# Float64 weights: the sign from GpSimd, the join and the elementwise work on VectorE, and other times for loads and conversions

## The chip, the cores and the metric

The kernel runs on one core of one Trainium2 chip. The metric is the device time of one execution in microseconds (us); the time of before is the median of three runs, 909.39 us (908.66 to 910.81). The engines are named as in the profile: PE is TensorE, DVE is VectorE, ACT is ScalarE, POOL is GpSimd and SP is SyncE. PEld is TensorE's loading of weights.

## The reference, cut to what matters

Three layers follow each other over 2304 tokens. The first is a masked attention (4 batches, 8 heads, 576 positions). The second is a feed-forward layer whose gate and output weights are drawn as float32 and divided by a square root that numpy holds in float64, so the weights reach the kernel as float64:

```python
xn = x / rms * rms_g
g = xn @ w_gate
silu = g * (1.0 / (1.0 + np.exp(-g)))
val = xn @ w_val
x = (silu * val @ w_out).astype(np.float32)
```

The third layer routes each token to one of eight experts. It is not touched by the change.

## The kernel before, in words

[...] The pieces of work:

- `load_w(n)` (L377) starts the load of weight n from ACT's queue. `next_load` (L413) calls it behind `mark`, the latest exp of the attention or tanh of the feed-forward layer, on ACT.
- `conv_a(n)` (L383): ACT scales the high word as a float32 (L388), and DVE shifts the low word right by 29 (L389).
- `conv_b(n)` (L391): DVE shifts the scaled word left by 3 and joins it with the low bits (L394), then takes the sign bit from the scaled word and joins it in (L398).
- `conv_c(n)` (L403): ACT rounds to the high part (L406), and POOL subtracts to get the low part (L407).
- These make a list of 73 pieces, `conv` (L420): a of 0, b of 0, then a of n together with c of n - 1, then b of n. `convert()` (L427) takes the next piece, and passes over every fourth call; with `LEAD` it calls for loads ahead of the pieces. `weight(n)` (L439) takes pieces until weight n is there.

The buffers of `raw`, of the work words `wk` and of the finished weight lie in a row of slots: weight n is loaded into slot n + 3, its work words lie in slot n + 2, the finished parts in slot n. So the work words of n replace the raw words of n - 1, and must wait until these have been read.

The order of the program is this. 24 units of attention run first (`att_sequence`, L250): each is scores with mask and exp (L155), division by the sum (`norm`, L201, its multiplication on POOL at L208), transposition and output. When the loop at L684 has reached unit 7 (26 pieces of attention), three more pieces and `rms0`, the normalisation of the first 256 tokens, follow. Then the flow (L1059) goes through 108 steps, 12 slices of the feed-forward width for each of nine chunks of 256 tokens; the first two chunks alternate and share the weights as they come, so that the 36 weights are wanted within the first 24 steps. A step is `gate_val` twice (24 matmuls of 256 columns, L458 to L460), `gelu_post` (L462: tanh on ACT, two DVE operations L467 and L468, rounding on ACT at L471, the rest `hl` on POOL at L472), `ff_out` of the step two before (six matmuls of 512 columns, L483 to L485), and three calls of `slot` (L722). A slot calls `next_load` and `convert` and then one piece of the attention or of the routing. `rms` for the later chunks subtracts on POOL for chunks 1 and 2 and on DVE otherwise (L353). Experts follow from the middle of the last chunk on.

The order on each engine isn't the program's: a planner places the instructions of this part in the order in which its own cost model finds them ready, the earlier of the program first. On the chip each engine then works through its list in that fixed order.

Of the kernel before, what the change touches and what calls it, by code (L numbers as in the profile page):

```python
# [10 lines left out]
F32 = mybir.dt.float32  # L11
# [5 lines left out]
ALU = mybir.AluOpType  # L17
# [29 lines left out]
def moe_kernel(  # L47
# [17 lines left out]
    V, A, G, T, SP = nc.vector, nc.scalar, nc.gpsimd, nc.tensor, nc.sync  # L65
# [81 lines left out]
    def attention(u, banks):  # L147

        b, p, g = units[u]
        local = p < 2  # L150
        n, t0, nq, nk = geometry(u)
        k0 = n * nq if local else n * nq + LQ - SQ
        st = {}

        def scores():  # L155
            t = qkv_t.pop((u, 0))
            pr = pp.tile([128, 4, LK], F32, tag="pr", name="pr", bufs=3)
            mx = sm.tile([128, 4], F32, tag="mx", name="mx")
            sd = sm.tile([128, 4], F32, tag="sd", name="sd")
            sps = banks("s")  # L160
            if n_fill[0] < 16:
                n_fill[0] += 1
                fill(sps[:, 384:], 10)
            sps = sps[:, :4 * LK].rearrange("p (t k) -> p t k", k=LK)
            for i in range(n):
                for h in range(2):
                    hp = slice(64 * h, 64 * h + 64)
                    T.matmul(
                        sps[hp, i, :nk],
                        t[hp, i * nq:i * nq + LQ],  # L170
                        t[hp, k0 + i * nq:k0 + i * nq + nk],
                        start=True,
                        stop=True,
                    )
            for i in range(n):
                mask = m_str if not local else (m_loc0 if g == 0 and i == 0 else m_loc)
                pv = pr[:, i, :nk]
                V.tensor_tensor_reduce(  # L178
                    out=pv,
                    in0=sps[:, i, :nk],  # L180
                    in1=mask[:, :nk],
                    op0=ALU.add,
                    op1=ALU.min,
                    scale=-0.125,
                    scalar=3.0e38,
                    accum_out=mx[:, i:i + 1],
                )
                act = A.activation(  # L188
                    out=pv,
                    in_=pv,  # L190
                    func=AF.Exp,
                    bias=mx[:, i:i + 1],
                    scale=-1.0,
                    accum_out=None if u < 12 else sd[:, i:i + 1],
                )
                if not flow_on:
                    mark[0] = act
            st["p"] = pr, sd
            load_part(0)

        def norm():  # L201
            pr, sd = st["p"]
            pv, sl = pr[:, :n, :nk], sd[:, :n]
            if u < 12:
                V.tensor_reduce(out=sl, in_=pv, op=ALU.add, axis=AX.X)
            V.tensor_scalar(out=sl, in0=sl, scalar1=1e-9, scalar2=None, op0=ALU.add)
            V.reciprocal(out=sl, in_=sl)  # L207
            G.tensor_tensor(out=pv, in0=pv, in1=sl.unsqueeze(2).to_broadcast([128, n, nk]), op=ALU.mult)  # L208

        def transpose():  # L210
            pr, _ = st.pop("p")
            pt = banks("t").rearrange("p (t k) -> p t k", k=128)
            for i in range(n):
                T.transpose(pt[:nk, i], pr[:, i, :nk], ident)
            ptS = st["t"] = pp.tile([128, 4, 128], F32, tag="ptS", name="ptS", bufs=2)
            A.copy(ptS[:nk, :n], pt[:nk, :n])

        def output():
            t = qkv_t.pop((u, 1))
            ptS = st.pop("t")  # L220
            ot = banks("o")
            for i in range(n):
                for h in range(2):
                    T.matmul(
                        ot[64 * h:64 * h + 64, i * nq:(i + 1) * nq],
                        t[:nk, i, 64 * h:64 * h + 64],
                        ptS[:nk, i, 64 * h:64 * h + nq],
                        start=True,
                        stop=True,
                    )  # L230
            if local:
                x = x_t[b, p, g] = xt_p.tile([128, n * LQ], F32, tag=f"x{g}", name=f"x{g}", bufs=2)
                A.copy(x, ot[:, :n * LQ])
            else:
                if g == 0:
                    x_t[b, p] = xt_p.tile([128, S], F32, tag="xs", name="xs", bufs=4)
                x = x_t[b, p].rearrange("p (j c) -> p c j", c=CLS)
                c0, c1 = 3 * t0, min(3 * (t0 + n), CLS)
                A.copy(x[:, c0:c1], ot[:, :(c1 - c0) * LEN].rearrange("p (c j) -> p c j", j=LEN))
            load_part(1)  # L240
            n_out[0] = u + 1


        if local and b > 0:
            output.after = (S * (b - 1) + LQ * (t0 + n) - 1) // CH
        elif not local and b > 1:
            output.after = (S * (b - 1) - 1) // CH
        return scores, norm, transpose, output
# [42 lines left out]
    def rms(j):  # L291
# [49 lines left out]
        def scale(q):  # L341
            y = tmp_p.tile([128, 2, CH], F32, tag="tmp", name="y")
            h = xn_p.tile([128, 2, CH], F32R, tag=f"xh{q}", name=f"xh{q}")
            l = xn_p.tile([128, 2, CH], F32R, tag=f"xl{q}", name=f"xl{q}")
            for c in range(2):
                p = 2 * q + c
                for src, o, n in segments(j, p):
                    yv, gp = y[:, c, o:o + n], g_sb[:, p:p + 1]
                    V.scalar_tensor_tensor(
                        out=yv, in0=src, scalar=gp, in1=st["r"][:, o:o + n], op0=ALU.mult, op1=ALU.mult  # L350
                    )
            A.copy(h, y)
            (G if j in (1, 2) else V).tensor_tensor(out=l, in0=y, in1=h.bitcast(F32), op=ALU.subtract)  # L353
            st[f"x{q}"] = [h[:, 0], h[:, 1]], [l[:, 0], l[:, 1]]
            if "x0" in st and "x1" in st:
                xn_t[j] = tuple(st["x0"][i] + st["x1"][i] for i in range(2))
                normed[0] = j
# [9 lines left out]
    w_t = {}  # L367
    raw_t = {}
    wk_t = {}
    sign = -(1 << 31)  # L370

    def w_slot(n, shape, dtype, name):
        if n < NP:
# [9 lines left out]
    def conv_a(n):  # L383
        wk, raw = w_slot(n + 2, [128, 2, 512], I32, "wk"), raw_t[n]
        wk_t[n] = wk


        A.activation(out=wk[:, 0].bitcast(F32), in_=raw[:, :, 1].bitcast(F32), func=AF.Copy, scale=2.0**-112)  # L388
        V.tensor_scalar(out=wk[:, 1], in0=raw[:, :, 0], scalar1=29, scalar2=None, op0=ALU.logical_shift_right)  # L389

    def conv_b(n):  # L391
        wk = wk_t[n]
        raw_t.pop(n)
        V.scalar_tensor_tensor(  # L394
            out=wk[:, 1], in0=wk[:, 0], scalar=3, in1=wk[:, 1],
            op0=ALU.logical_shift_left, op1=ALU.bitwise_or,
        )
        V.scalar_tensor_tensor(  # L398
            out=wk[:, 0], in0=wk[:, 0], scalar=sign, in1=wk[:, 1],
            op0=ALU.bitwise_and, op1=ALU.bitwise_or,  # L400
        )

    def conv_c(n):  # L403
        wk = wk_t.pop(n)[:, 0].bitcast(F32)
        w = w_t[n] = w_slot(n, [128, 2, 512], F32R, "wf")
        A.copy(w[:, 0], wk)  # L406
        G.tensor_tensor(out=w[:, 1], in0=wk, in1=w[:, 0].bitcast(F32), op=ALU.subtract)  # L407

    n_wl = [0]
    mark = [None]  # L410
# [12 lines left out]
    conv += [lambda: conv_c(NP - 1)]  # L423
    conv.reverse()

    cv = [0]
    def convert(n=1):  # L427
        cv[0] += 1
        if cv[0] % 4 == 0:
            return  # L430
        while n and conv:
            while n_wl[0] < NP and 2 * (n_wl[0] - LEAD) <= 2 * NP + 1 - len(conv):
                next_load()
            conv.pop()()
            n -= 1

    LEAD = 2

    def weight(n):  # L439
        while n not in w_t:  # L440
# [21 lines left out]
    def gelu_post(j, f):  # L462
# [6 lines left out]
        h = sl_p.tile([128, CH], F32R, tag="hh", name="hh")  # L469
        l = sl_p.tile([128, CH], F32R, tag="hl", name="hl")  # L470
        A.copy(h, t)  # L471
        G.tensor_tensor(out=l, in0=t, in1=h.bitcast(F32), op=ALU.subtract)  # L472
        hm_t[j, f] = h, l

    def ff_out(j, f):
# [186 lines left out]
        )  # L662
    V.tensor_tensor(out=bsel, in0=bsel, in1=bt, op=ALU.add)

    P0, P1, P2, P3, P4, P5 = 3, 3, 1, 4, 1, 3
    stage = [0]
    turn = {"s": 0, "t": 0, "o": 0}

# [15 lines left out]
    while n_out[0] < 8:  # L684
        aux.pop()()
        n_p += 1
        if n_p % P0 == 0 and n_wl[0] < P1 and n_p >= 15:
            next_load()
    for _ in range(P5):
        aux.pop()()  # L690
    flow_on.append(1)
    for f in rms0:
        f()
# [28 lines left out]
    def slot():  # L722
        s = now[0]
        now[0] += 1
        if s % P2 == 0:
            next_load()
        convert()
        if s in plan:
            for f in plan[s]:
                f()  # L730
        else:
            pop_aux()
# [495 lines left out]
```

## Time and profile before

| what | value |
|---|---|
| median of three runs | 909.39 us |
| the profiled execution, its own time | 910.19 us |
| its span, first to last instruction | 908.4 us |
| PE busy | 865.5 us (95%) |
| DVE busy | 503.7 us (55%) |
| ACT busy | 402.0 us (44%) |
| POOL busy | 223.7 us (25%) |
| bytes read from HBM | 91.58 MB |
| mean granted clock of TensorE | 0.974 |

The span is the part of the execution that the trace covers, and 1.8 us lie around it. Busy shares are averages over stages of different kinds: the attention at the start, the flow, and the experts. A busy PE need not be at its peak, because matmuls overlap in a pipeline; the number of matmuls in a stretch tells more.

### The profile page before, as it was taken

What the parts mean: (1) busy time and instruction counts of PE and PEld (TensorE: products, weight loads), DVE (VectorE), ACT (ScalarE), POOL (GpSimd) and SP (SyncE); (2) the same over time, 40 slices, a digit from 0 to 9 for tenths busy, and PEclk for the clock granted to TensorE, in tenths of its full rate; (3) what the DMA queues carried; (4) which work ended last, traced back from release to release, by engine and by line L of the source; (5) the groups of instructions that cost most, each with busy time, mean ns of one, the idle gap of its engine ahead of it and who ended that gap; (6) DMA issues with size and microseconds to landing.
All of it is one profiled execution on the core that took longest, in us unless ns stands there. A gap on an engine that the chain in (4) does not pass through costs nothing. (4 is left out here: it accounts for less than half of the span.)

```text
span 908.4 us, 18299 instructions
## 1 busy us (share of the span) xinstructions
PE 865.5 (95%) x6912; PEld 774.5 (85%) x6912; DVE 503.7 (55%) x1489; ACT 402.0 (44%) x970; POOL 223.7 (25%) x246
## 2 busy tenths in 40 slices
PE   8888977899999999999999999999899999999995
PEld 7676866798888898899989999998789999999994
DVE  3679999733454353362442524437586666666650
ACT  4776655325445335343232232325265555554540
POOL 1335666521112112112112111113031111111100
PEclk8889998999999999999999999999999999999998
DMA  4736860001212102110000000005187752676000
GB/s 122 221 101 235 290 243 25 1 1 39 76 32 63 52 1 60 55 35 21 24 10 17 9 1 24 1 26 207 40 303 206 226 176 74 208 233 189 30 25 19
DMA packets 33016, 84.48 MB, mean 93 GB/s; under 512 B 5122, under 2 KB 12850, under 8 KB 32920
## 3 DMA queue, kind: packets, MB, share of 16 engines
q1 hardware_dynamic: 24216, 54.89, 19.6%
q10 hardware_dynamic: 5184, 18.88, 5.8%
q0 software_dynamic: 3520, 9.45, 3.1%
q8 instruction: 58, 0.95, 0.5%
q14 instruction: 38, 0.31, 0.1%
HBM read 91.58 MB, written 10.49 MB: 112 GB/s over the span
## 5 line engine op out<-in xcount | busy, mean ns | idle before, releaser
L458 PE MATMUL gv<-xh,wf 128*128 128x256 f32 x864 | 253.4, 294 | 11.2 <-DVE t L468 10.7
L460 PE MATMUL gv<-xh,wf 128*128 128x256 f32 x864 | 247.9, 287 | 0.0
L459 PE MATMUL gv<-xl,wf 128*128 128x256 f32 x864 | 247.2, 286 | 0.1
L458 PEld LDWEIGHTS gv<-xh,wf 128*128 128x128 f32 x864 | 166.3, 193 | 21.1 <-DVE t L468 13.9
L459 PEld LDWEIGHTS gv<-xl,wf 128*128 128x128 f32 x864 | 166.5, 193 | 3.2 <-POOL xl L353 0.4
L460 PEld LDWEIGHTS gv<-xh,wf 128*128 128x128 f32 x864 | 166.5, 193 | 0.8 <-issue 0.2
L472 POOL TENSOR_TENSOR hl<-t,hh 128x256 fp32r<-128x256 f32 x108 | 86.2, 798 | 325.8 <-ACT hh L471 266.7
L946 DVE TENSOR_TENSOR l<-stg,h 128x1024 fp32r<-128x1024 f32 x88 | 107.5, 1227 | 38.7 <-ACT h L945 38.2
L467 DVE SCALAR_TENSOR_TENSOR t<-t,gv 128x256 f32<-128x256 f32 x108 | 45.2, 418 | 148.6 <-ACT t L466 148.0
L945 ACT CAST h<-stg 128x1024 fp32r<-128x1024 f32 x88 | 91.7, 1047 | 38.6 <-PE o L1002 27.6
L466 ACT ACTIVATE t<-gv 128x256 f32<-128x256 f32 x108 | 41.3, 383 | 141.2 <-PE gv L460 131.2
L471 ACT CAST hh<-t 128x256 fp32r<-128x256 f32 x108 | 43.7, 404 | 82.6 <-PE o L485 33.2
L483 PE MATMUL o<-wf,hh 128*128 128x512 f32 x192 | 76.9, 402 | 0.4 <-ACT hh L471 0.2
L484 PE MATMUL o<-wf,hh 128*128 128x512 f32 x192 | 75.9, 396 | 0.0
L485 PE MATMUL o<-wf,hl 128*128 128x512 f32 x192 | 75.6, 398 | 0.0
L1000 PE MATMUL o<-h,hT 128*128 128x512 f32 x176 | 71.1, 404 | 0.0
L1002 PE MATMUL o<-h,hT 128*128 128x512 f32 x176 | 69.1, 392 | 0.0
L1001 PE MATMUL o<-l,hT 128*128 128x512 f32 x176 | 68.7, 391 | 0.0
L929 POOL DMA_INDIRECT xg<-rows_d,gi x22 | 25.3, 1148 | 160.9 <-issue 140.3
L188 ACT ACTIVATE pr<-pr,mx 128x54 f32<-128x54 f32 (+1 forms) x160 | 52.7, 347 | 21.3 <-DVE mx L178 21.2
L407 POOL TENSOR_TENSOR wf<-wk,wf 128x512 fp32r<-128x512 f32 x36 | 51.0, 1421 | 32.0 <-ACT wf L406 30.7
L208 POOL TENSOR_TENSOR pr<-pr,sd 128x216 f32<-128x216 f32 (+4 forms) x48 | 30.0, 625 | 95.2 <-DVE sd L207 63.2
(206 smaller groups left out, 1699.1 us busy)
## 6 DMA issues: line engine op xcount, KB each, us to landing
stg<-in SPq DMA_DIRECT2D x96, 512.0 KB
raw<-in ACTq DMA_DIRECT2D x36, 512.0 KB
rows_d<-x SPq DMA_DIRECT2D x18, 256.5 KB
qk<-in SPq DMA_DIRECT2D x16, 221.0 KB
qk<-in SPq DMA_DIRECT2D x8, 272.0 KB
v<-in SPq DMA_DIRECT2D x16, 108.0 KB
qk<-in SPq DMA_DIRECT2D x8, 208.0 KB
v<-in SPq DMA_DIRECT2D x8, 192.0 KB
```

Source lines behind the costliest of these rows:

```text
L458: T.matmul(dst, wh[:, ks], xh[k], start=(k == order[0]), stop=False)
L459: T.matmul(dst, wh[:, ks], xl[k], start=False, stop=False)
L460: T.matmul(dst, wl[:, ks], xh[k], start=False, stop=(k == order[3]))
L472: G.tensor_tensor(out=l, in0=t, in1=h.bitcast(F32), op=ALU.subtract)
L483: T.matmul(o, h[:, ms], wh, start=(f == 0), stop=False)
L484: T.matmul(o, h[:, ms], wl, start=False, stop=False)
L485: T.matmul(o, l[:, ms], wh, start=False, stop=(f == NF - 1))
L945: A.copy(h, lt["stg", i])
L946: V.tensor_tensor(out=l, in0=lt["stg", i], in1=h.bitcast(F32), op=ALU.subtract)
L1000: T.matmul(ys[t][m], hh, w[0][:, c], start=(q == 0 and c == 0), stop=False)
L1001: T.matmul(ys[t][m], hh, w[1][:, c], start=False, stop=False)
L1002: T.matmul(ys[t][m], hl, w[0][:, c], start=False, stop=(q == 3 and c == 1))
```

## The change

The change moves the sign: POOL makes it in `conv_a` from the high word, as the integer of 0 or -2^31. DVE then needs two operations and no separate shift. Four subtractions and multiplications go from POOL to DVE, and the calls of `next_load` and `convert` come at other places: a load at every second piece of the attention, a piece of the conversion at every second one after the tenth, with no passing over in `convert`, and `LEAD` of 4.

```diff
@@ norm
-            G.tensor_tensor(out=pv, in0=pv, in1=sl.unsqueeze(2).to_broadcast([128, n, nk]), op=ALU.mult)
+            V.tensor_tensor(out=pv, in0=pv, in1=sl.unsqueeze(2).to_broadcast([128, n, nk]), op=ALU.mult)
@@ rms, scale
-            (G if j in (1, 2) else V).tensor_tensor(out=l, in0=y, in1=h.bitcast(F32), op=ALU.subtract)
+            V.tensor_tensor(out=l, in0=y, in1=h.bitcast(F32), op=ALU.subtract)
@@ conv_a
-        V.tensor_scalar(out=wk[:, 1], in0=raw[:, :, 0], scalar1=29, scalar2=None, op0=ALU.logical_shift_right)
+        G.tensor_scalar(
+            out=wk[:, 1], in0=raw[:, :, 1].bitcast(F32), scalar1=0.0, scalar2=-(2.0**31),
+            op0=ALU.is_lt, op1=ALU.mult,
+        )
@@ conv_b
-        wk = wk_t[n]
-        raw_t.pop(n)
+        wk, raw = wk_t[n], raw_t.pop(n)
         V.scalar_tensor_tensor(
-            out=wk[:, 1], in0=wk[:, 0], scalar=3, in1=wk[:, 1],
-            op0=ALU.logical_shift_left, op1=ALU.bitwise_or,
+            out=wk[:, 1], in0=raw[:, :, 0], scalar=29, in1=wk[:, 1],
+            op0=ALU.logical_shift_right, op1=ALU.bitwise_or,
         )
         V.scalar_tensor_tensor(
-            out=wk[:, 0], in0=wk[:, 0], scalar=sign, in1=wk[:, 1],
-            op0=ALU.bitwise_and, op1=ALU.bitwise_or,
+            out=wk[:, 0], in0=wk[:, 0], scalar=3, in1=wk[:, 1],
+            op0=ALU.logical_shift_left, op1=ALU.bitwise_or,
         )
@@ conv_c
-        G.tensor_tensor(out=w[:, 1], in0=wk, in1=w[:, 0].bitcast(F32), op=ALU.subtract)
+        V.tensor_tensor(out=w[:, 1], in0=wk, in1=w[:, 0].bitcast(F32), op=ALU.subtract)
@@ convert
-        cv[0] += 1
-        if cv[0] % 4 == 0:
-            return
         while n and conv:
-    LEAD = 2
+    LEAD = 4
@@ gelu_post
-        G.tensor_tensor(out=l, in0=t, in1=h.bitcast(F32), op=ALU.subtract)
+        V.tensor_tensor(out=l, in0=t, in1=h.bitcast(F32), op=ALU.subtract)
@@ order
-    P0, P1, P2, P3, P4, P5 = 3, 3, 1, 4, 1, 3
+    P0, P1, P2, P3, P4, P5 = 2, 10, 2, 4, 1, 3
...
-        if n_p % P0 == 0 and n_wl[0] < P1 and n_p >= 15:
+        if n_p % P0 == 0:
             next_load()
+        if n_p > P1 and n_p % P2 == 0:
+            convert()
     for _ in range(P5):
         aux.pop()()
+        convert()
...
-        if s % P2 == 0:
-            next_load()
+        next_load()
         convert()
```

## Rows read from the trace of the kernel before

**Rows 1.** Stages: from:to length, busy PE, PEld, DVE, ACT, POOL (xinstructions), clock, DMA share, GB/s.

```profile
9.00:29.00 20.00, 17.33 (x271) 14.46 (x268) 9.34 (x70) 11.74 (x38) 3.93 (x7) 0.83 0.51 144
29.00:96.00 67.00, 56.25 (x593) 46.78 (x594) 56.57 (x215) 48.30 (x162) 30.14 (x30) 0.85 0.58 189
96.00:173.00 77.00, 63.63 (x449) 55.32 (x448) 76.93 (x118) 41.68 (x90) 50.46 (x41) 0.93 0.42 148
173.00:209.00 36.00, 35.58 (x255) 32.54 (x255) 11.16 (x29) 9.69 (x24) 10.12 (x12) 1.00 0.01 4
209.00:634.00 425.00, 424.87 (x3546) 382.41 (x3544) 181.63 (x780) 162.88 (x491) 82.22 (x111) 1.00 0.13 40
```

**Rows 2.** The same view for L458 alone (PE, PEld, clock, DMA share, GB/s).

```profile
9.00:96.00 87.00, 13.72 (x40) 9.49 (x40) 0.84 0.56 179
96.00:173.00 77.00, 29.78 (x96) 19.79 (x96) 0.93 0.42 148
173.00:209.00 36.00, 18.22 (x64) 12.05 (x64) 1.00 0.01 4
```

**Rows 3.** Waits of the whole span: us in total, times, longest us.

```profile
DVE l L946 <- ACT h L945: 38.2, 64, 2.7
POOL wf L407 <- ACT wf L406: 30.7, 22, 4.1
PE gv L458 <- DVE t L468: 10.7, 8, 2.3
```

**Rows 4.** Timeline of DVE, 119.6 to 122.7 us: start us, length us.

```profile
119.64 0.68 DVE L394 SCALAR_TENSOR_TENSOR wk<-wk 128x512 int32<-128x512 int32 x1
120.24 0.41 DVE L389 TENSOR_SCALAR wk<-raw 128x512 int32<-128x512 int32 x1
120.57 0.41 DVE L304 TENSOR_TENSOR sq<-sq 128x256 f32<-128x256 f32 x1
120.91 0.41 DVE L467 SCALAR_TENSOR_TENSOR t<-t,gv 128x256 f32<-128x256 f32 x1
121.24 1.43 DVE L398 SCALAR_TENSOR_TENSOR wk<-wk 128x512 int32<-128x512 int32 x1
```

**Rows 5.** Timeline of POOL in the same stretch.

```profile
120.76 1.36 POOL L407 TENSOR_TENSOR wf<-wk,wf 128x512 fp32r<-128x512 f32 x1 [2.55 <-ACT wf L406]
```

**Rows 6.** Groups on DVE, 0 to 209 us: busy us, mean ns | idle before.

```profile
L398 DVE SCALAR_TENSOR_TENSOR wk<-wk 128x512 int32<-128x512 int32 x36 | 36.4, 1011 | 0.0
L394 DVE SCALAR_TENSOR_TENSOR wk<-wk 128x512 int32<-128x512 int32 x36 | 31.5, 875 | 0.4 <-ACT wk L388 0.3
L389 DVE TENSOR_SCALAR wk<-raw 128x512 int32<-128x512 int32 x36 | 28.4, 790 | 7.0 <-DMA raw<-in 7.0
...
L329 DVE TENSOR_TENSOR nt<-nr 128x2 f32<-128x2 f32 x9 | 4.6, 512 | 0.1
...
L331 DVE SCALAR_TENSOR_TENSOR nr<-nt,nr 128x2 f32<-128x2 f32 x9 | 3.1, 342 | 0.2
```

**Rows 7.** Line L329: duration ns shortest/median/longest, first and last start.

```profile
L329 DVE TENSOR_TENSOR nt<-nr x27: 129/161/1254, 51.5 to 569.7; 128x2 f32<-128x2 f32 x27
```

**Rows 8.** Groups on POOL, 0 to 209 us.

```profile
L407 POOL TENSOR_TENSOR wf<-wk,wf 128x512 fp32r<-128x512 f32 x36 | 51.0, 1421 | 32.0 <-ACT wf L406 30.7 <-issue 1.3
L472 POOL TENSOR_TENSOR hl<-t,hh 128x256 fp32r<-128x256 f32 x24 | 22.6, 940 | 27.8 <-ACT hh L471 26.8 <-POOL hl L472 1.0
L208 POOL TENSOR_TENSOR pr<-pr,sd 128x216 f32<-128x216 f32 (+4 forms) x24 | 15.7, 656 | 48.6 <-DVE sd L207 27.7 <-ACT xs L239 8.6 <-ACT pr L188 8.0
L353 POOL TENSOR_TENSOR xl<-y,xh 128x512 fp32r<-128x512 f32 x4 | 6.2, 1579 | 3.3 <-ACT xh L352 3.3
```

**Rows 9.** Line L407, the same columns.

```profile
L407 POOL TENSOR_TENSOR wf<-wk,wf x36: 1255/1364/1746, 34.1 to 172.5; 128x512 fp32r<-128x512 f32 x36
```

**Rows 10.** The loads of `raw` on ACT's queue, the same columns.

```profile
L380 ACTq DMA_DIRECT2D raw<-in x36: 334/435/1788, 23.8 to 137.8; - x36
```

**Rows 11.** The page's costliest groups, L946 alone: busy us, mean ns | idle before.

```profile
L946 DVE TENSOR_TENSOR l<-stg,h 128x1024 fp32r<-128x1024 f32 x88 | 107.5, 1227 | 38.7 <-ACT h L945 38.2
```

More of the change, by code (lines that the diff above doesn't have):

```diff
@@ L369, in moe_kernel @@
     wk_t = {}
-    sign = -(1 << 31)
     def w_slot(n, shape, dtype, name):
@@ L424, in moe_kernel @@
     conv.reverse()
-    cv = [0]
     def convert(n=1):
-        cv[0] += 1
-        if cv[0] % 4 == 0:
-            return
         while n and conv:
```

## The prediction

> **What bounds the kernel now.** I read the busy time by stage first. From 209 to 634 us PE is busy for 424.87 of 425 us, so there only PE counts; before 209 us it isn't [rows 1]. A step has eight L458 matmuls. PE does 96/8 = 12 steps between 96 and 173 us, which is 6.4 us each, and 64/8 = 8 steps in the next 36 us, 4.5 us each; by 209 us it has done 200/8 = 25 steps [rows 2]. What slows the 77 us is DVE, busy for 76.93 of them [rows 1]; PE waits for its L468 to free a bank of PSUM [rows 3]. So the question is when 25 steps are done, with all 36 conversions, which PE can't start without. Whatever that moment moves, the end moves with it, because behind it PE is full and no changed line of the conversion runs any more. PE's own limit: at 4.5 us, the 77 us would hold 17 steps, so some 5 steps or 23 us are to be had.
>
> **DVE's account before.** From 9 us on, when the attention's work reaches it, up to 209 us DVE is busy for 9.3 + 56.6 + 76.9 + 11.2 = 154.0 us of 200 [rows 1]. The 46.0 us it is idle are 10.7 from 9 to 29, 10.4 from 29 to 96, and 24.8 after 173 us, when the conversions are over: 3.1 us in each of eight steps.
>
> Part of the busy time is no work. The two-input operation L394 of 512 elements takes 0.68 us when it is free, and so can L398, which has the same form; L398 took 1.43 us when a POOL instruction stood in the same stretch [rows 4, 5]. L389 takes 0.41 us free [rows 4]. Against the means [rows 6] that is (1011 - 680) + (875 - 680) + (790 - 410) = 906 ns per weight, 32.6 us for 36. L329 and L331, 161 ns in the median [rows 7] (L331 taken as the like), lose (512 - 161) + (342 - 161) = 532 ns, nine times, 4.8 us [rows 6]. In all 37.4 us are lost beside 51.0 + 22.6 + 15.7 + 6.2 = 95.5 us of POOL [rows 8]: 0.39 us for each us that POOL works.
>
> **The change, part by part,** in DVE time from start to start up to the 25th step; pitches from [rows 4]: 0.60 us for a two-input operation of 512 elements, 0.33 for L389 and for 256 elements.
>
> - Lost time beside POOL goes: 37.4 off.
> - L389 goes: 36 x 0.33 = 11.9 off. The two joining operations stay two, 0.60 each; that one now reads the strided raw word I cost at nothing, since L389 reads the same words and takes less time than they do [rows 4]. If the stride halved the rate it would add 36 x 0.6 = 22 us.
> - The low part of the weight: 36 x 0.60 = 21.6 on.
> - `hl`: 24 x 0.33 = 7.9 on. `norm`: 24 of 162 to 384 elements, taken as 256: 7.9 on. `xl`: 4 x 0.60 = 2.4 on (counts from [rows 8]).
> - The sign on POOL is an operation that the trace doesn't show. POOL's subtraction of the same width takes 1.255 us at its shortest [rows 9]. The sign reads one input instead of two: half of that, 0.63 us, is the low end; it does two operations and makes an integer: twice, 2.5 us, is the high end. I take 1.0 us, as L407 is the nearest row and the reads are halved. DVE loses 36 x 1.0 x 0.39 = 14.0 us (ends 8.8 and 35).
>
> The Trainium skill (GPSIMD Engine Reference, Performance versus the Vector engine) gives POOL's best loop as 1.8 cycles an element, 769 ns for 512; by that estimate the sign would cost DVE 36 x 0.77 x 0.39 = 10.8 us and the whole come out 3 us earlier. No row here shows it.
>
> Busy: 154.0 - 37.4 - 11.9 + 21.6 + 7.9 + 7.9 + 2.4 + 14.0 = 158.5 us. DVE has thus 4.5 us more to do than before, and a gain can only come from its idle time.
>
> - **Loads and conversions earlier.** Before, the first load is issued at 23.8 us [rows 10], and DVE waits 7.0 us for raw words [rows 6]. By the program, 13 loads instead of 3 come before unit 7 is out, from the first exp on, and 8 + 3 + 5 = 16 pieces of the conversion lie ahead of the flow. Of the 21.1 us idle between 9 and 96 us, the 7.0 go, and 4 of the 10.7 before 29 us: 10.1 stay. (Ends: 5 if nearly all are filled, 21 if none.) On ACT's queue the loads are the same 36 at 0.435 us [rows 10]; eight of them move into the attention, 3.5 us of issue, beside some three more weights' rounding and scaling. ACT is 48.3 of 67 us busy there [rows 1], so I cost that at nothing; if the room is gone the attention stretches (rival four). SP's queue and POOL's have no load moved.
> - **A wait that moves.** The subtraction waits for ACT's rounding. POOL waited for it 30.7 us in 22 cases [rows 3]; now DVE does, with gelu and the next conversion queued behind, and PE behind those. The ends are 0, where the planner has put other work between, and 30.7. The nearest row is the same pair on DVE, L946 behind L945: 38.2 us in 88 operations [rows 11], 0.43 each, so 36 x 0.43 = 15.6. That DVE had little else to do; here there is other work, so I take half, 8 us.
> - **The conversions' end.** It came after 136/8 = 17 steps [rows 2]. With 73 - 16 = 57 pieces left at three a step the program ends them at step 19. Two steps leave the idle stretch: 2 x 3.1 = 6.2 of 24.8, 18.6 stay. If the planner pulls the conversions further ahead this sign turns: each step earlier costs 3.1.
> - After 209 us `hl` and `norm` add at most 83 x 0.33 = 27 and 24 x 0.33 = 8 us to 181.6 of 425 us of DVE; PE hides them. The lag of two steps before `hl` is used, 9 us, covers its queueing.
>
> Idle: 10.1 + 8 + 18.6 = 36.7. With 158.5 busy, 25 steps are done 195.2 instead of 200 us after the ninth, at 204.2 instead of 209 us: 4.8 us earlier. The profiled execution takes 910.19 us, its span 908.4 and 1.8 around it; it lies 0.8 above the median of 909.39. So 905.4 for it, **904.5 us** for the median. A difference under 0.2%, 1.8 us, can't be told from none.
>
> **The rivals.**
>
> 1. *More of the idle time is used.* The sign takes 0.63 us (5.2 less), the wait is hidden (8 less), another 5 us of the attention's idle time are filled: 23 us earlier, 886.5 us, where PE's own limit lies. For it: DVE was idle for 46.0 of 200 us. Against it: conversions sit in one queue with the attention.
> 2. *DVE waits for the rounding* (slower). Its place is the subtraction of `conv_c`. At the 0.60 us of one wait of L946 (38.2/64) [rows 3], 36 waits are 21.5 instead of 8 us: 8.7 us later than now, 918 us. It decides from 8 + 4.8 = 12.8 us of waits on. For it: 30.7 us on POOL. Against it: pieces of other work lie between.
> 3. *POOL's sign holds DVE off for its whole length* (slower). L398 lost 0.75 of the 1.36 us of the POOL instruction beside it [rows 4, 5], more than the mean of 0.39. If each sign operation costs DVE its whole 1.0 us, that is 36 instead of 14: 17 us later than now, 926.5 us. It decides from 0.52 us per sign on. The Trainium skill (SBUF — State Buffer, SBUF: two separate sides) has a pair of ports shared by the two engines as an exclusive lock, held for the whole instruction by whoever starts first, against operations with two SBUF inputs; by that rule the long L398 is such a case. Against it: before, POOL held the pair almost three times as long, and lost DVE only 0.39 of it; L467 and L468, which read PSUM, lie between.
> 4. *The attention stretches by what is saved.* Loads of 0.5 MB compete with those of q, k and v, and conversions delay masks and exps, so the flow starts some 5 us later: no change, 909.4 us. That would also be the picture if the planner left the conversions where they were, so that only the loads had moved.
>
> **How the numbers follow.** The forecast, 899 to 907.5, has 0.38, rival one 0.17, rival two 0.18, rival three 0.13, rival four 0.14. Faster: 0.38 + 0.17 = 0.55; same 0.14; slower 0.31. The forecast's own range is 899 to 907.5. The range from 886 to 920 takes in rivals one, two and four and the low part of three; the rest, with PE's limit below and the full waits above, is some 0.15.
>
> **What would show it.** In the changed profile: POOL's sign operation near 1.0 us; the joining operations near 0.7 to 0.8 us in the mean instead of 0.88 and 1.01; first conversions before 20 us; no DVE wait for raw words; DVE's wait for the rounding near 8 us; DVE idle for some 37 us from 9 us until 25 steps are done, at 204 us; steps behind that at the old pace. It would be wrong if PE after step 25 were no longer full, if the sign took over 2 us, or if the flow began more than 5 us later without more conversions done by then.

## The result, and the profile after

The changed kernel takes 901.0 us (median of four runs, 898.1 to 905.0) against 910.1 for the kernel before, beside which it ran: a ratio of 0.9907, 95% interval 0.9884 to 0.9931. The forecast was 904.5. The profiled execution of after is the slowest of its four, 905.04 us with a span of 903.2, so the two traces differ by 5.2 us and the medians by 9.1. A weight arrives as float64, in pairs of 32-bit words (`raw`); two joins on DVE make a float32 of them, ACT rounds it to the high part, and the low part is the rest. Lines up to 369 keep their numbers; behind them, the first join is L396, the second L400, the sign L389, ACT's scaling L387 and rounding L408, the low part L409, the gate matmul L456, gelu L465 and L466, `hl` L470.

Busy time of the whole span after, from the page: DVE has 28 us more than before, POOL 95 less.

```profile
PE 865.0 (96%) x6912; PEld 777.1 (86%) x6912; DVE 531.5 (59%) x1649; ACT 402.1 (45%) x970; POOL 128.7 (14%) x86
```

The stages of after, in the columns of [rows 1], the fourth cut at 202 us:

```profile
9.00:29.00 20.00, 14.97 (x197) 11.98 (x195) 13.21 (x76) 11.85 (x37) 6.83 (x3) 0.73 0.83 268
29.00:96.00 67.00, 51.60 (x571) 41.89 (x569) 59.89 (x229) 48.61 (x154) 32.82 (x15) 0.75 0.55 174
96.00:173.00 77.00, 74.86 (x592) 68.50 (x591) 63.66 (x142) 43.66 (x107) 38.78 (x18) 0.97 0.36 129
173.00:202.00 29.00, 29.00 (x215) 27.02 (x215) 12.87 (x42) 7.63 (x19) 0.00 (x0) 1.00 0.02 5
209.00:634.00 425.00, 424.76 (x3551) 382.93 (x3549) 213.42 (x886) 162.86 (x491) 4.21 (x4) 1.00 0.12 40
```

Two things turned round. From 96 to 173 us DVE is no longer the full engine (63.7 of 77 us instead of 76.93); PE is (74.9 instead of 63.63). And up to 96 us PE does less than before: 768 matmuls instead of 864, at a granted clock of 0.73 and 0.75 instead of 0.83 and 0.85 (means over the two levels of the clock, 1.00 or 2.4 GHz and 0.50 or 1.2 GHz). The gate matmul alone (PE, PEld, clock, DMA share, GB/s), to be read against [rows 2]:

```profile
9.00:96.00 87.00, 7.37 (x21) 5.33 (x21) 0.75 0.61 196
96.00:173.00 77.00, 36.37 (x127) 24.52 (x126) 0.97 0.36 129
9.00:202.00 193.00, 59.01 (x200) 39.85 (x200) 0.88 0.42 140
```

At eight to a step, 2.6 steps instead of 5 are done by 96 us, then 15.9 instead of 12, and the 25th at 202 us, where before it came at 208 (the 209 of the prediction, read a microsecond finer). Behind the 25th step nothing changed: 908.4 - 208 = 700.4 us before, 903.2 - 202 = 701.2 after. In all twelve experiments this rest lies between 697.8 and 701.6 us, so the moment of the 25th step tells the time of each profiled run.

Groups of DVE in after, 0 to 202 us (busy us, mean ns | idle before, releaser):

```profile
L400 DVE SCALAR_TENSOR_TENSOR wk<-wk 128x512 int32<-128x512 int32 x36 | 27.3, 757 | 0.1
L409 DVE TENSOR_TENSOR wf<-wk,wf 128x512 fp32r<-128x512 f32 x36 | 26.9, 746 | 7.3 <-ACT wf L408 7.1
L396 DVE SCALAR_TENSOR_TENSOR wk<-raw,wk 128x512 int32<-128x512 int32 x36 | 24.6, 684 | 0.2
L329 DVE TENSOR_TENSOR nt<-nr 128x2 f32<-128x2 f32 x9 | 2.3, 255 | 0.1
```

POOL's one group of work there (0 to 209 us):

```profile
L389 POOL TENSOR_SCALAR wk<-raw 128x512 int32<-128x512 f32 x36 | 78.4, 2179 | 84.2 <-DVE wk L396 28.6 <-DMA raw<-in 19.6 <-DVE sd L206 8.3
```

The first join, which reads the strided raw word, takes 684 ns in the mean, a free two-input operation's time, and L329 went from 512 to 255 ns [rows 6]. The sign takes POOL 2.18 us, more than twice what was forecast, and yet DVE hardly feels it. The first join can't run beside a sign here: it waits for its own, and the next one waits for it. The other operations can. Two signs in the timeline of POOL (start, length):

```profile
34.45 1.96 POOL L389 TENSOR_SCALAR wk<-raw 128x512 int32<-128x512 f32 x1 [3.09 <-DVE wk L396]
38.56 2.15 POOL L389 TENSOR_SCALAR wk<-raw 128x512 int32<-128x512 f32 x1 [2.15 <-DMA qk<-in]
```

and what DVE did beside them:

```profile
34.69 0.96 DVE L409 TENSOR_TENSOR wf<-wk,wf 128x512 fp32r<-128x512 f32 x1
...
36.10 0.68 DVE L400 SCALAR_TENSOR_TENSOR wk<-wk 128x512 int32<-128x512 int32 x1
...
38.80 1.14 DVE L409 TENSOR_TENSOR wf<-wk,wf 128x512 fp32r<-128x512 f32 x1
```

L409 started 0.24 us into each sign and ended at 35.65 and 39.94 us, while the signs ran to 36.41 and 40.71. It lost 0.28 and 0.46 us; L400, shown beside the first, lost nothing.

**Where the time now goes.** The flow alternates two chunks, and the second can't start before its `rms` is done: sum, a root of thirteen small operations on DVE (L323 to L331, three rounds of Newton's formula), then PE spreads the result (L337). DVE's timeline in after over the end of that root:

```profile
82.27 0.15 DVE L323 TENSOR_SCALAR na<-mx 128x2 f32<-128x2 f32 x1
...
86.73 0.69 DVE L409 TENSOR_TENSOR wf<-wk,wf 128x512 fp32r<-128x512 f32 x1
87.34 0.15 DVE L331 SCALAR_TENSOR_TENSOR nr<-nt,nr 128x2 f32<-128x2 f32 x1
87.41 0.69 DVE L396 SCALAR_TENSOR_TENSOR wk<-raw,wk 128x512 int32<-128x512 int32 x1
88.01 0.15 DVE L329 TENSOR_TENSOR nt<-nr 128x2 f32<-128x2 f32 x1
88.13 0.69 DVE L400 SCALAR_TENSOR_TENSOR wk<-wk 128x512 int32<-128x512 int32 x1
88.74 0.60 DVE L330 TENSOR_TENSOR nt<-nt,na 128x2 f32<-128x2 f32 x1
89.37 0.16 DVE L331 SCALAR_TENSOR_TENSOR nr<-nt,nr 128x2 f32<-128x2 f32 x1
```

The planner put five operations of the conversion, and others of gelu, mask and `norm`, between the thirteen, and three of the thirteen took 0.49 to 0.60 us instead of some 0.16, each with a sign on POOL beside it. The root takes 7.1 us from the start of its first operation to the start of its last. Before it took 4.5:

```profile
66.53 0.16 DVE L323 TENSOR_SCALAR na<-mx 128x2 f32<-128x2 f32 x1 [3.01 <-PE mx L317]
...
71.06 0.15 DVE L331 SCALAR_TENSOR_TENSOR nr<-nt,nr 128x2 f32<-128x2 f32 x1
```

In after PE stands still for 3.2 us until the root is done, from its timeline:

```profile
89.59 0.49 PE L337 MATMUL mx<-cs,nr 128*128 128x128 f32 x2 [3.16 <-DVE nr L331]
```

Then PE fills. Stretches of 10 us, PE busy, clock, DMA share, GB/s, first of before:

```profile
121.00:131.00 10.00, 7.35 (x51) 0.83 0.70 260
...
141.00:151.00 10.00, 6.83 (x31) 0.66 0.00 0
...
161.00:171.00 10.00, 7.20 (x47) 1.00 0.00 0
```

Such stretches of after, all engines from PE to POOL ahead of the clock:

```profile
101.00:111.00 10.00, 7.86 (x62) 6.82 (x62) 8.42 (x23) 5.93 (x18) 5.93 (x3) 0.83 0.92 342
111.00:121.00 10.00, 10.00 (x95) 8.92 (x94) 8.05 (x21) 6.58 (x19) 4.81 (x3) 1.00 0.98 354
...
151.00:161.00 10.00, 10.00 (x75) 9.43 (x74) 8.42 (x17) 4.74 (x11) 5.95 (x3) 1.00 0.01 2
```

From 111 us on after's PE is full up to step 25 and beyond, at a clock of 1.00, although the conversions go on to 166 us. So before is limited by the conversions on DVE until 173 us. After, as the traces read, is limited by the moment at which the second chunk can start, 89.4 us instead of 71.1, and by PE behind it; between 89 and 111 us PE also waits 2.1 us for gelu (L466) and works in part at the lower clock (the last section).

### The profile page after: what moved, and what is told of

It is laid out like the page before. It is cut to its first block, busy times and chain, and to the rows that moved or that the text cites. A ratio compares the mean times of both kernels' runs of the same rounds, so it can differ in the third digit from the quotient of the medians.

```text
span 903.2 us, 18170 instructions
## 1 busy us (share of the span) xinstructions
PE 865.0 (96%) x6912; PEld 777.1 (86%) x6912; DVE 531.5 (59%) x1649; ACT 402.1 (45%) x970; POOL 128.7 (14%) x86
## 5 line engine op out<-in xcount | busy, mean ns | idle before, releaser
L456 PE MATMUL gv<-xh,wf 128*128 128x256 f32 x864 | 250.9, 291 | 3.4 <-DVE t L466 2.1
L458 PE MATMUL gv<-xh,wf 128*128 128x256 f32 x864 | 245.8, 285 | 0.0
L456 PEld LDWEIGHTS gv<-xh,wf 128*128 128x128 f32 x864 | 164.9, 191 | 10.6 <-DVE t L466 2.8
L458 PEld LDWEIGHTS gv<-xh,wf 128*128 128x128 f32 x864 | 164.9, 191 | 0.4
L946 DVE TENSOR_TENSOR l<-stg,h 128x1024 fp32r<-128x1024 f32 x88 | 107.3, 1224 | 40.1 <-ACT h L945 40.0
L465 DVE SCALAR_TENSOR_TENSOR t<-t,gv 128x256 f32<-128x256 f32 x108 | 45.3, 419 | 109.0 <-ACT t L464 108.0
L389 POOL TENSOR_SCALAR wk<-raw 128x512 int32<-128x512 f32 x36 | 78.4, 2179 | 84.2 <-DVE wk L396 28.6
L470 DVE TENSOR_TENSOR hl<-t,hh 128x256 fp32r<-128x256 f32 x108 | 46.4, 429 | 36.0 <-ACT hh L469 33.2
L979 PE MATMUL s<-xh,h 128*128 128x256 f32 x176 | 49.7, 282 | 0.0
```

Of the source, the lines that this page charges most:

```text
L389: G.tensor_scalar(out=wk[:, 1], in0=raw[:, :, 1].bitcast(F32), scalar1=0.0, scalar2=-(2.0**31), op0=ALU.is_lt, op1=ALU.mult,)
L456: T.matmul(dst, wh[:, ks], xh[k], start=(k == order[0]), stop=False)
L458: T.matmul(dst, wl[:, ks], xh[k], start=False, stop=(k == order[3]))
L946: V.tensor_tensor(out=l, in0=lt["stg", i], in1=h.bitcast(F32), op=ALU.subtract)
```

## The experiments

The experiments' times are medians, each with its ratio to the kernel before on the same chip (910.3, 910.9 and 910.7 us in three groups). The letters of theories are explained in the texts on record. The planner makes its lists anew for every kernel, so each edit can also move work that it doesn't name; no run holds the lists fixed.

### The engines or the order?

**The engines alone**, with before's calls of loads and conversions:

```diff
+    cv = [0]
     def convert(n=1):
+        cv[0] += 1
+        if cv[0] % 4 == 0:
+            return
...
-    LEAD = 4
+    LEAD = 2
...
-    P0, P1, P2, P3, P4, P5 = 2, 10, 2, 4, 1, 3
+    P0, P1, P2, P3, P4, P5 = 3, 3, 1, 4, 1, 3
...
-        if n_p % P0 == 0:
+        if n_p % P0 == 0 and n_wl[0] < P1 and n_p >= 15:
             next_load()
-        if n_p > P1 and n_p % P2 == 0:
-            convert()
     for _ in range(P5):
         aux.pop()()
-        convert()
```

> The engines of the changed kernel in the order of the kernel before (loads, conversions, passing over and LEAD as before). Theory A, DVE's account: the time that VectorE loses beside GpSimd goes (37 us to about 5), the moved work adds 28, the idle 46 us stay: 25 steps of the flow at about 205 us, 904 to 907 us. Theory B, the gain is the order's: 908 to 911 us. Theory C, the gain is the engines' and the order costs (the flow began 11 us later in the changed kernel): 892 to 899 us.

901.6 us, 0.9903 (0.9886 to 0.9919): as fast as the whole change, and faster than the account of the prediction gives. No theory's range holds it. The 25th step is done at 199 us, the last conversion at 189.

**The order alone**: before's engines with the reverse of that diff.

> The engines of the kernel before in the order of the changed one. Theory A: VectorE has the busy time of before with its 37 us lost beside GpSimd, and some 8 us less idle time: 902 to 906 us. Theory B: 899 to 902 us, all of the gain. Theory C: the attention stretches and nothing pays for it: 912 to 920 us.

922.5 us, 1.0132 (1.0115 to 1.0149): 12 us slower than before, in theory C's direction and beyond its range. 14 weights instead of 5 are ready when the flow starts, but it starts at 75.8 us instead of 61.0, and the second chunk's root ends at 91.0 instead of 71.1. So the engines bring the gain; the order takes 12 us from before's engines and nothing from after's.

### What does POOL's work cost DVE, kind by kind?

**One line of before: the low part on DVE**, the sign, the calls of loads and conversions and all else as before:

```diff
-        G.tensor_tensor(out=w[:, 1], in0=wk, in1=w[:, 0].bitcast(F32), op=ALU.subtract)
+        V.tensor_tensor(out=w[:, 1], in0=wk, in1=w[:, 0].bitcast(F32), op=ALU.subtract)
```

> The kernel before with one line changed: the low part of the weights on VectorE. The sign stays there, so VectorE has four operations for a weight. Theory A by terms: 51 us of two-input work leaves GpSimd, 51 x 0.4 = 20 us of losses less, 36 x 0.60 = 22 more work and some 7 of waits: 911 to 919 us. Theory S, what GpSimd's low part cost was more than its losses in VectorE's durations show (the kernel with it back on GpSimd lost 7.7 us of 9): 899 to 905 us.

899.2 us, 0.9875 (0.9847 to 0.9903): this line alone brings what the whole change brings, as theory S had it. Its groups on DVE, 0 to 205 us, by before's line numbers:

```profile
L394 DVE SCALAR_TENSOR_TENSOR wk<-wk 128x512 int32<-128x512 int32 x36 | 27.7, 769 | 0.5 <-ACT wk L388 0.5
L398 DVE SCALAR_TENSOR_TENSOR wk<-wk 128x512 int32<-128x512 int32 x36 | 26.2, 729 | 0.0
L407 DVE TENSOR_TENSOR wf<-wk,wf 128x512 fp32r<-128x512 f32 x36 | 26.2, 727 | 0.8 <-ACT wf L406 0.7
...
L389 DVE TENSOR_SCALAR wk<-raw 128x512 int32<-128x512 int32 x36 | 16.2, 450 | 4.7 <-DMA raw<-in 4.7
```

Against [rows 6] the three old operations take (875 - 769) + (1011 - 729) + (790 - 450) = 728 ns less per weight, 26.2 us for 36, which is just what L407 takes on DVE: by these four lines DVE does POOL's 51.0 us of work at no cost, but without a gain either. Per us of that POOL work, these operations had lost 26.2/51.0 = 0.51 us. The gain stands in DVE's whole busy time up to the 25th step, here of before (208 us) and of this kernel (199 us):

```profile
9.00:208.00 199.00, 171.79 (x1559) 148.27 (x1557) 154.00 (x430) 111.02 (x312) 94.64 (x88) 0.91 0.41 136
9.00:199.00 190.00, 166.49 (x1564) 145.66 (x1562) 143.47 (x468) 111.23 (x313) 46.13 (x52) 0.89 0.42 142
```

DVE is busy for 10.5 us less and idle for as long as before (45.0 and 46.5 us). Some 6 us of the saving are shorter small operations, those of the roots above all; the rest is that more operations overlap the one before. PE stands 10.7 us for the second chunk's root in this kernel, so it may not yet be at its best.

**The low part back on POOL** in after (the same line, G for V):

> The changed kernel with the weights' low part (conv_c) back on GpSimd, alone. Theory A by the ratio of the prediction: VectorE loses 36 x 0.60 = 22 us of work and 7 of waits, and gains 36 x 1.255 x 0.39 = 18 of losses beside GpSimd: 892 to 899 us. Rival E, the two-input operations on GpSimd were the whole cost of before, at more than 0.39 us each: 904 to 910 us, with the mean of the joining operations again near 0.9 to 1.0 us.

908.7 us, 0.9987 (0.997 to 1.0004): the gain is gone, as rival E had it. The two joins, in its groups for 0 to 205 us:

```profile
L396 DVE SCALAR_TENSOR_TENSOR wk<-raw,wk 128x512 int32<-128x512 int32 x36 | 39.3, 1092 | 2.3 <-POOL wk L389 2.2
L400 DVE SCALAR_TENSOR_TENSOR wk<-wk 128x512 int32<-128x512 int32 x36 | 32.4, 900 | 0.4
```

They lose (1092 - 684) + (900 - 757) = 551 ns per weight, 19.8 us beside 47.9 us of L409 on POOL: 0.41. Moving the low part is thus what matters in the change, from both sides.

**The sign back on DVE**, as before in three operations, so POOL has nothing to do:

```diff
-        G.tensor_scalar(
-            out=wk[:, 1], in0=raw[:, :, 1].bitcast(F32), scalar1=0.0, scalar2=-(2.0**31),
-            op0=ALU.is_lt, op1=ALU.mult,
-        )
+        V.tensor_scalar(out=wk[:, 1], in0=raw[:, :, 0], scalar1=29, scalar2=None, op0=ALU.logical_shift_right)
```

(and the two joins of before, the second of which takes the sign).

> The changed kernel with the sign back on VectorE (shift, join, sign: three operations as before), nothing left on GpSimd in this stage. Theory A: 36 x 0.33 = 12 us more on VectorE, some 5 us of losses beside GpSimd gone: 25 steps 4 to 7 us later, 904 to 908 us. Rival D, the chain from a sign operation of 2.2 us to the join and from there to the next sign sets the pace of the conversions: without it they end earlier and the time falls to 890 to 898 us.

905.9 us, 0.9938 (0.9922 to 0.9955), 4.9 us above after and in theory A's range, though the two intervals overlap a little. It is the clean measure of free DVE operations: the joins take 684 and 683 ns, L405 (the low part) 686, the shift 421. Against them after's L400 and L409 lose (757 - 683) + (746 - 686) = 134 ns per weight, 4.8 us beside 78.4 us of signs: 0.06 us per us, not 0.39. That isn't only because the first join never meets a sign in after: with own slots for the raw words (below), where it needn't wait so, the three lose (703 - 684) + (750 - 683) + (727 - 686) = 127 ns, again 0.06.

**A shorter sign**: the high word times zero as a float, one operation, no integer to make.

```diff
-            out=wk[:, 1], in0=raw[:, :, 1].bitcast(F32), scalar1=0.0, scalar2=-(2.0**31),
-            op0=ALU.is_lt, op1=ALU.mult,
+            out=wk[:, 1].bitcast(F32), in0=raw[:, :, 1].bitcast(F32), scalar1=0.0, scalar2=None, op0=ALU.mult,
```

> The changed kernel with a shorter sign: GpSimd multiplies the high word as a float by 0.0, whose result has the sign bit alone, one operation and no integer. The sign should take 0.7 to 1.3 us instead of 2.18. Theory D, the chain counts: 36 times 1 us shorter, 894 to 899 us. Rival H, the sign lies beside other work: 899 to 903 us. Theory L, a sign holds VectorE off for its length: the joining operations' mean falls from 0.73 to 0.69 us, no more than 2 us in all.

903.7 us, 0.9929 (0.9901 to 0.9956): no gain, nearest to rival H. Its sign (ns minimum/median/maximum, first and last start), and the join that lost most (0 to 205 us):

```profile
L389 POOL TENSOR_SCALAR wk<-raw x36: 1519/1606/3093, 13.8 to 155.6; 128x512 f32<-128x512 f32 x36
L399 DVE SCALAR_TENSOR_TENSOR wk<-wk 128x512 int32<-128x512 int32 x36 | 30.7, 853 | 0.1
```

A quarter off the median (2160 in after), and the time doesn't follow: what the sign takes on POOL doesn't set the end. DVE lost more beside this sign, not less as theory L had it: (853 - 683) + (738 - 686) = 222 ns per weight, 8.0 us beside 62.5 us of signs, 0.13. Why the shorter sign costs more stays open.

**`norm`, `hl` and `xl` back on POOL** in after:

```diff
-            V.tensor_tensor(out=pv, in0=pv, in1=sl.unsqueeze(2).to_broadcast([128, n, nk]), op=ALU.mult)
+            G.tensor_tensor(out=pv, in0=pv, in1=sl.unsqueeze(2).to_broadcast([128, n, nk]), op=ALU.mult)
...
-            V.tensor_tensor(out=l, in0=y, in1=h.bitcast(F32), op=ALU.subtract)
+            (G if j in (1, 2) else V).tensor_tensor(out=l, in0=y, in1=h.bitcast(F32), op=ALU.subtract)
...
-        V.tensor_tensor(out=l, in0=t, in1=h.bitcast(F32), op=ALU.subtract)
+        G.tensor_tensor(out=l, in0=t, in1=h.bitcast(F32), op=ALU.subtract)
```

> The changed kernel with norm, hl and xl back on GpSimd as before, and only the low part of the weights left on VectorE. Theory E, each two-input operation of GpSimd costs VectorE about as much as it saves there, or more: 904 to 908 us, with the joining operations near 0.8 us in the mean. Theory A by the ratio 0.39: VectorE is spared 18 us and loses 45 x 0.39 = 17: no change, 899 to 903 us.

894.4 us, 0.9823 (0.9792 to 0.9855): faster than both kernels, which neither theory expected. Its conversions on DVE lose more than after's, as its groups for 0 to 205 us show:

```profile
L396 DVE SCALAR_TENSOR_TENSOR wk<-raw,wk 128x512 int32<-128x512 int32 x36 | 33.5, 930 | 2.4 <-POOL wk L389 1.5 <-DMA v<-in 0.5
L400 DVE SCALAR_TENSOR_TENSOR wk<-wk 128x512 int32<-128x512 int32 x36 | 31.1, 865 | 0.3
L409 DVE TENSOR_TENSOR wf<-wk,wf 128x512 fp32r<-128x512 f32 x36 | 28.1, 783 | 7.8 <-ACT wf L408 7.6
```

(930 - 684) + (865 - 757) + (783 - 746) = 391 ns per weight, 14.1 us beside some 47 us of the three on POOL: 0.30. If conversions still set the end, it should be no faster than after. What became shorter is the root of the second chunk; DVE's timeline over it, and behind it PE's line that waits for the root:

```profile
79.26 0.16 DVE L323 TENSOR_SCALAR na<-mx 128x2 f32<-128x2 f32 x1
...
81.39 0.16 DVE L331 SCALAR_TENSOR_TENSOR nr<-nt,nr 128x2 f32<-128x2 f32 x1
81.58 0.16 DVE L329 TENSOR_TENSOR nt<-nr 128x2 f32<-128x2 f32 x1
81.78 0.16 DVE L330 TENSOR_TENSOR nt<-nt,na 128x2 f32<-128x2 f32 x1
82.67 0.42 DVE L465 SCALAR_TENSOR_TENSOR t<-t,gv 128x256 f32<-128x256 f32 x1 [0.73 <-ACT t L464]
83.01 0.15 DVE L331 SCALAR_TENSOR_TENSOR nr<-nt,nr 128x2 f32<-128x2 f32 x1
...
83.83 0.38 PE L337 MATMUL mx<-cs,nr 128*128 128x128 f32 x2
```

No conversion stands in it; it ends at 83.0 instead of 89.4 us, and PE has other work until then. The flow's start isn't the reason: it comes at 72.6 us here and at 70.4 in after.

**Only `norm` on DVE**, `hl` and `xl` on POOL as in the last kernel (its first line with V for G):

> The changed kernel with hl and xl back on GpSimd and norm left on VectorE (894.4 us had all three back). Theory Q, hl is what VectorE shouldn't have in its queue, since it waits there for ScalarE's rounding: 893 to 897 us. Rival R, norm is: it stands in VectorE's queue in the attention, 24 x 0.4 us, where the flow's start is at stake: 899 to 902 us.

900.5 us, 0.9892 (0.9865 to 0.9919), 6.1 us slower than with `norm` on POOL. The time was rival R's, the reason given for it was not seen: the flow starts earlier (66.4 instead of 72.6 us). What came back is the wait for the root: PE stands 3.3 us for it, and it takes 7.2 instead of 3.7 us. Its profiled run took 896.5 us, level with that of the last kernel (896.3), so this pair of traces shows only 2 us of the 6, and the wait for the root as the cause is argued from it, not shown.

### Is it the pace of the conversions?

**Own slots for the raw words**, so that work words of n no longer wait for the raw words of n - 1:

```diff
-            raw = w_slot(n + 3, [128, 512, 2], I32, "raw")
+            raw = w_slot(n + 4, [128, 512, 2], I32, "raw")
```

> The changed kernel with the raw words of weight n in slot n + 4 instead of n + 3, so that the work words of n no longer replace the raw words of n - 1: GpSimd's sign of n needn't wait for VectorE's join of n - 1. Theory D, the chain sign, join, sign sets the pace: GpSimd's wait for the join (28.6 us) goes, the conversions end some 15 us earlier, 893 to 898 us. Rival, the place of the conversions in VectorE's queue sets it and the chain is hidden: 899 to 903 us.

904.0 us, 0.9931 (0.9911 to 0.9951). POOL's wait for the join falls from 28.6 to 7.0 us and the last conversion comes at 151 instead of 166 us, but no time is gained, against theory D.

**No conversions called in the attention**:

```diff
-        if n_p > P1 and n_p % P2 == 0:
-            convert()
     for _ in range(P5):
         aux.pop()()
-        convert()
```

> The changed kernel with its early loads, but none of the eleven conversion pieces among the attention's first 29. Theory F, the conversions stretch the attention (they sit in VectorE's and ScalarE's queues between mask and exp): the first gate matmul comes at 62 to 66 us instead of 71, time 897 to 901 us. Rival G, the loads stretch it (they compete with those of q, k and v): it stays at 69 to 73 us, and with fewer conversions done by then 902 to 908 us.

900.3 us, 0.9882 (0.9847 to 0.9917), after's time. The planner pulled conversions forward all the same: 11 weights are ready at the first gate matmul, as in after, and that comes at 66.5 instead of 70.4 us. So what stretches the attention couldn't be told apart this way.

**The same in the fastest kernel:**

> The swap alone (norm, hl, xl on GpSimd) with the changed order, but no conversion pieces among the attention's first 29. Theory N: no difference to 894.4 us, 892 to 897 us. Rival P: the flow starts some 5 us earlier and the whole ends earlier with it: 887 to 891 us.

894.3 us, 0.9829 (0.9801 to 0.9856): no difference to 894.4 either (theory N).

**The fastest kernel's engines in before's order:**

> Only the swap of the conversion (sign to GpSimd, low part to VectorE), with norm, hl and xl on GpSimd and the order of the kernel before. Theory N, with these engines the order makes no difference, as the two earlier pairs differ by under 1 us: 892 to 898 us. Rival P, the earlier start of the flow in the old order (61 instead of 73 us) is worth something here: 884 to 890 us.

905.5 us, 0.9944 (0.9925 to 0.9963), which neither theory expected: 11 us slower than in the new order. With five weights ready at the first gate matmul, the last conversion comes at 196 us, 4.2 us a weight, and PE waits on the way. Against the engines alone (901.6), which stand in the same order, `norm`, `hl` and `xl` on POOL cost 4 us here; in the new order they bring 7. What three moves are worth depends on the order that they stand in, and why they cost time here stays open.

### The traces together

Root is the second chunk's, on DVE, from the start of L323 to that of the last L331; then how long PE stands for it ("none" where it has other work). The last column is from the root's end to the 25th step. Each row is the profiled run of its kernel, which isn't its median.

| kernel | median us | root us | PE's wait | last conversion | 25 steps | rest |
|---|---|---|---|---|---|---|
| before | 910 | 66.5 to 71.1 | none | 173 | 208 | 137 |
| order alone | 922.5 | 82.5 to 91.0 | 1.1 | 165 | 218 | 127 |
| engines alone | 901.6 | 68.4 to 72.5 | 0.8 | 189 | 199 | 126 |
| fastest, before's order | 905.5 | 69.8 to 72.7 | none | 196 | 207 | 134 |
| low part on POOL | 908.7 | 82.6 to 90.5 | 3.1 | 183 | 207 | 116 |
| after | 901.0 | 82.3 to 89.4 | 3.2 | 166 | 202 | 113 |
| own slots | 904.0 | 78.1 to 84.7 | none | 151 | 200 | 115 |
| no conversions in attention | 900.3 | 78.2 to 85.3 | 3.4 | 162 | 198 | 113 |
| sign on DVE | 905.9 | 86.3 to 99.5 | 8.5 | 167 | 209 | 110 |
| shorter sign | 903.7 | 82.3 to 89.6 | 5.2 | 161 | 200 | 110 |
| `norm` on DVE | 900.5 | 78.3 to 85.5 | 3.3 | 166 | 196 | 110 |
| fastest | 894.4 | 79.3 to 83.0 | none | 170 | 194 | 111 |
| fastest, none in attention | 894.3 | 76.1 to 79.9 | none | 167 | 191 | 111 |
| before, low part on DVE | 899.2 | 72.4 to 88.0 | 10.7 | 179 | 199 | 111 |

In all fourteen traces PE has done exactly two steps (16 of the first gate matmuls) when the root ends, and the other 23 come behind it: at 4.5 us each they are 103.5 us, and PE has the rest of the attention to do beside them. In the last nine rows the rest is 110 to 115 us, while the 25th step lies anywhere from 191 to 209: there it follows the end of the root. In the first four rows the rest is 126 to 137 us: there PE starves on the way, waiting for weights or for DVE; the low part on POOL lies between. The change moved the kernel from one limit to the other. It fits that faster conversions bring nothing in after (own slots, shorter sign). With the sign on DVE the root takes 13.1 us and PE stands 8.5 us for it, in a profiled run that lies above its median (911.2 us). Own slots fit less well: PE doesn't stand for the root there, and the median is no better than after's.

This is read from fourteen traces. No run moved the root and nothing else, so it is shown as where the time lies, not by an experiment of its own. Why the planner interleaves the root in some kernels and not in others stays open too.

## Why the prediction was right, and where it wasn't

The time came out within the range, 3.5 us below the forecast, in the direction given the most chance. The account was made for the profiled execution, for which it gives 905.4 us; that of after took 905.04. So near a hit is in part luck: two errors of 9 and 7 us below nearly cancel. What the median gained beyond that, some 4 us, stands in no trace.

- **The 25th step decides.** Right: behind it every kernel takes 698 to 702 us.
- **DVE's account.** Busy was forecast to rise from 154.0 to 158.5 us; up to the 25th step it is 13.21 + 59.89 + 63.66 + 12.87 = 149.6 us, 8.9 less. "A gain can only come from its idle time" is the sentence that failed. The term behind it is the sign: 4.8 instead of 14.0 us, below the low end of 8.8. Those 9.2 us are as much as the whole error; the other terms together came out right, though not each of them: `norm` and `hl` took 469 and 445 ns in the mean, where 410 were taken. Two sizes were wrong at once: the sign takes 2.18 us, not 1.0, and costs DVE 0.06 us for each us, not 0.39. A sign of over 2 us was one of the three marks by which the prediction called itself wrong; it came, and yet the longer sign cost DVE less, not more.
- **The ratio 0.39** is a mean over kinds of POOL work that cost DVE quite different amounts: 0.41 to 0.51 for the two-input low part, 0.30 for `norm`, `hl` and `xl`, 0.06 for the one-input sign and 0.13 for its shorter form. The mean hid that moving the low part alone is worth the whole gain.
- **Strided raw words at nothing**: right, 684 ns.
- **The wait for ACT's rounding**: right, 7.1 us for the 8 taken; rival two didn't come. `hl` on DVE waits for its own rounding too, 4.1 us, which the sum left out.
- **Idle time** was forecast as 36.7 us and is 193 - 149.6 = 43.4: (20 - 13.21) + (67 - 59.89) = 13.9 instead of 10.1 up to 96 us, 13.3 instead of 8 up to 173, and 16.1 instead of 18.6 behind it. The two errors, 8.9 of busy and 6.7 of idle time, nearly cancel: 193 us in all for the 195.2 forecast. And DVE's idle time from 111 us on costs nothing, since PE is full there; the account adds up, but it no longer says what sets the end.
- **The conversions' end** came at step 16.9, not 19: the planner did pull them ahead.
- **The attention "costed at nothing"** failed: the flow starts at 70.4 instead of 61.0 us and the second chunk's root ends 18 us later, as rival four had it in kind. The prediction asked whether more conversions would be done by then; 11 are, not 5. That later start isn't by itself what limits after, since the fastest kernel's flow starts at 72.6 us. The end of the root is, as the traces read: 83.0 us there, 89.4 in after. That chain stood in no term of the sum.
- **Rival three**, the sign holding DVE off for its whole length, didn't come: L409 finished while the sign still ran. The Trainium skill (SBUF — State Buffer, SBUF: two separate sides) has the shared pair of ports locked for a whole instruction, between a DVE operation with two SBUF inputs and a GpSimd one that reads SBUF. POOL's two-input low part agrees: L398 ended 0.55 us after it [rows 4, 5], so most of its free 0.68 us lay behind POOL's end. For the one-input sign the measurement differs: no L400 or L409 of after took over 1.18 us, at most 0.5 us lost beside some 2 us. The Trainium skill's best loop rate (GPSIMD Engine Reference, Performance versus the Vector engine) gave the estimate of 769 ns for the sign; the median here, 2160 ns, is 2.8 times that.

## What to carry to other kernels

Price what one engine's work costs its neighbour by kind, from single instructions in the timeline: here the two-input subtraction cost DVE about half its length, and the one-input sign 0.06 to 0.13 of its own. When one bound is lifted, look for the first moment from which the fullest engine never stops again: here conversions that ended 15 us sooner behind it brought nothing, and a short dependent chain ahead of it is where the traces put the time. Work moved to an engine whose order a planner writes can land between the links of such a chain, so try the parts of a change singly: one line of this one brought its whole gain, and taking three of its moves back brought 7 us more in its new order, though not in the old one.

## What was not expected of the hardware

- POOL's `tensor_scalar` of 512 elements from float32 to an integer took 1.95 to 2.49 us (the sign in after), and a single multiplication with a float result still 1.52 us or more, longer than its two-input subtraction (1255 ns at the shortest [rows 9]). Both forms of the sign read every second word.
- After a stand of PE the granted clock is lower for a while. In after it is 0.72 in the mean of the 10 us from 91 us on, behind the wait for the root. In stretches of 2 us it is at its lower level (0.50, 1.2 GHz) from 90 to 96 us, and at the upper one (1.00, 2.4 GHz) again from 98 us, PE having been nearly full since 92 us; behind PE's wait for gelu it falls once more, to 0.50 from 104 to 106 us. All engines from PE to POOL, clock, DMA share and GB/s:

```profile
90.00:92.00 2.00, 1.13 (x5) 0.50 (x4) 1.68 (x7) 0.74 (x2) 0.63 (x1) 0.50 0.00 0
98.00:100.00 2.00, 2.00 (x19) 2.00 (x19) 1.78 (x4) 0.62 (x1) 0.94 (x1) 1.00 0.00 0
```

A late root may cost time in this way too; that wasn't measured by itself.
